# Cosformer attention and a mixer MLP on one core: program order by hand, batches in pairs of nine token chunks

## The chip, the cores and the metric

The kernel runs on one core of a Trainium2 chip. The metric is the device time of one launch in microseconds; the kernel before takes 447.08 us, the median of three runs (444.23 to 447.29). PE is TensorE (PEld its weight loads), DVE VectorE, ACT ScalarE, POOL GpSimd, and SP the engine whose queue issues every DMA of both kernels.

## The reference

Eight batches, eight heads, 576 tokens, head size 64; the model width is 512, the hidden width 2048, the rank 32. All inputs are float32.

```python
r = np.maximum(x, 0.0)                                   # phi of q and k
return np.concatenate([r * c, r * s], axis=-1)           # 64 -> 128 features
...
kv = np.einsum('bhsf,bhsd->bhfd', k_p, v)
z = np.sum(k_p, axis=2)
num = np.einsum('bhsf,bhfd->bhsd', q_p, kv)
den = np.einsum('bhsf,bhf->bhs', q_p, z)[..., None] + 1e-06
...
h = xt @ U @ V                                           # xt: x with tokens last
u = x + h.transpose(0, 2, 1)
ch = np.maximum(u @ w_ch1, 0.0) @ w_ch2
return (u + ch).astype(np.float32)
```

c and s are the cosine and sine of a token's angle, which depends on its position alone, and x is num/den with the heads side by side.

## The kernel before

Each batch is cut into five token chunks, four of 128 and one of 64. For a batch, `loads` fetches q, k and v of a chunk with one DMA each (tokens on partitions; every head of a token is a run of 64 floats, 256 bytes, in memory), casts v on POOL into `v_ext` with a column of ones (line 172), and writes the scaled relu of k and q on ACT, cosine and sine half apart (lines 173 to 185).

`front` is attention and low-rank mixing. For each chunk and head one PE transpose of q_p goes into a PSUM tile of 128x128 (line 218), which DVE copies out by itself (line 222). The state kv accumulates over chunks, four heads to a tile (line 236), and is cast by DVE (line 243). x is four matmuls of 65 columns (line 258); DVE adds 1e-6 to the four denominators and inverts them (lines 266 and 270), ACT scales the four heads one by one (line 273). A = U^T x is five matmuls of 512 columns (line 288), va = V^T A one per chunk (line 304); DVE adds x (line 308), and four transposes (line 314) with a DVE copy each (line 319) make uT.

`back` is the MLP. The first layer has 16 slices of the hidden width by two token groups of 288, four matmuls each (line 337), with the relu on ACT (line 344). The second layer takes a token chunk at a time, 16 matmuls of 512 columns (line 360), five chunks per batch, the last of 64 tokens; DVE adds u (line 368), and SP stores (line 372).

A scheduler sets the order on each engine from the order of the thunks and from dependencies. The main loop at the end mixes the thunks of `front(b)` evenly among those of `back(b - 1)`, with the loads of batch b + 1 after the 32nd thunk; in batch 0 the weight loads and their casts on ACT (lines 111 and 126) are mixed in instead. Transposes have two PSUM buffers, attention accumulators two, and a shared tag of four holds the other matmul outputs.

Of the kernel before, what the change touches and what calls it, by code (L numbers as in the profile page):

```python
# [17 lines left out]
def kernel(  # L18
# [13 lines left out]
    B = 8  # L32
    H = 8
    S = 576
    D = 64
    P = 128
    DM = 512
    DH = 2048
    R = 32

    nchunk = 5
    csz = [128, 128, 128, 128, 64]
    cst = [0, 128, 256, 384, 512]

    const_pool = ctx.enter_context(tc.tile_pool(name="const", bufs=1))
    wpool = ctx.enter_context(tc.tile_pool(name="w", bufs=1))
    bpool = ctx.enter_context(tc.tile_pool(name="bat", bufs=2))
    ps = ctx.enter_context(tc.tile_pool(name="ps", bufs=2, space=bass.MemoryType.PSUM))

    ident_bf = const_pool.tile([P, P], BF16)  # L50
    make_identity(nc, ident_bf)

    iota = const_pool.tile([P, nchunk], FP32)
    nc.gpsimd.iota(
        out=iota,
        pattern=[[128, nchunk]],
        base=0,
        channel_multiplier=1,
        allow_small_or_imprecise_dtypes=True,
    )  # L60
    cosang = const_pool.tile([P, nchunk, 1], FP32)
    sinang = const_pool.tile([P, nchunk, 1], FP32)
    scale_ang = math.pi / (2.0 * S)
    halfpi = const_pool.tile([P, 1], FP32)
    nc.vector.memset(halfpi, math.pi / 2.0)
    nc.scalar.activation(out=sinang, in_=iota, func=AF.Sin, bias=0.0, scale=scale_ang)
    nc.scalar.activation(
        out=cosang, in_=iota, func=AF.Sin, bias=halfpi, scale=-scale_ang
    )

    stgA = const_pool.tile([P, DH], FP32)
    stgB = const_pool.tile([P, DH], FP32)
    stgs = [stgA, stgB]
    w1_bf = wpool.tile([P, 4, DH], BF16)
    w2_bf = wpool.tile([P, 16, DM], BF16)
    stgV = const_pool.tile([R, S], FP32)
    V_bf = wpool.tile([R, S], BF16)
    stgU = const_pool.tile([P, nchunk, R], FP32)
    U_bf = wpool.tile([P, nchunk, R], BF16)

    def weight_thunks():
        thunks = []

        def mk_uv():
            def t():
                for c in range(nchunk):
                    nc.sync.dma_start(
                        out=stgU[: csz[c], c, :], in_=moe_U[cst[c] : cst[c] + csz[c], :]
                    )
                nc.sync.dma_start(out=stgV, in_=moe_V)  # L90
                for c in range(nchunk):
                    nc.scalar.activation(
                        out=U_bf[: csz[c], c, :],
                        in_=stgU[: csz[c], c, :],
                        func=AF.Copy,
                        bias=0.0,
                        scale=1.0,
                    )
                nc.scalar.activation(
                    out=V_bf, in_=stgV, func=AF.Copy, bias=0.0, scale=1.0  # L100
                )

            return t

        thunks.append(mk_uv())

        def mk_w1(d):
            def t():
                s = stgs[d % 2]
                nc.sync.dma_start(out=s, in_=moe_w_ch1[d * 128 : d * 128 + 128, :])  # L110
                nc.scalar.activation(
                    out=w1_bf[:, d, :], in_=s, func=AF.Copy, bias=0.0, scale=1.0
                )

            return t

        for d in range(4):
            thunks.append(mk_w1(d))

        def mk_w2(j):  # L120
            def t():
                s = stgs[j % 2]
                nc.sync.dma_start(
                    out=s[:, 0:DM], in_=moe_w_ch2[j * 128 : j * 128 + 128, :]
                )
                nc.scalar.activation(
                    out=w2_bf[:, j, :], in_=s[:, 0:DM], func=AF.Copy, bias=0.0, scale=1.0
                )

            return t  # L130

        for j in range(16):
            thunks.append(mk_w2(j))
        return thunks

    st_kp = [None] * B
    st_vext = [None] * B
    st_qp = [None] * B
    st_qpT = [None] * B
    st_x = [None] * B  # L140
    st_kv = [None] * B
    st_A = [None] * B
    st_u = [None] * B
    st_uT = [None] * B
    st_hidT = [None] * B

    def loads(b):
        k_p = bpool.tile([P, nchunk, H, 2 * D], BF16, tag="k_p")
        v_ext = bpool.tile([P, nchunk, H, D + 1], BF16, tag="v_ext")
        q_p = bpool.tile([P, nchunk, H, 2 * D], BF16, tag="q_p")  # L150
        st_kp[b] = k_p
        st_vext[b] = v_ext
        st_qp[b] = q_p
        thunks = [lambda: nc.vector.memset(v_ext[:, :, :, D : D + 1], 1.0)]

        def mk(c):
            sz = csz[c]
            st = cst[c]
            def t():
                q_st = bpool.tile([P, H, D], FP32, tag="q_st")  # L160
                k_st = bpool.tile([P, H, D], FP32, tag="k_st")
                v_st = bpool.tile([P, H, D], FP32, tag="v_st")
                nc.sync.dma_start(
                    out=q_st[:sz], in_=q[b].rearrange("h s d -> s h d")[st : st + sz]
                )
                nc.sync.dma_start(
                    out=k_st[:sz], in_=k[b].rearrange("h s d -> s h d")[st : st + sz]
                )
                nc.sync.dma_start(
                    out=v_st[:sz], in_=v[b].rearrange("h s d -> s h d")[st : st + sz]  # L170
                )
                nc.gpsimd.tensor_copy(out=v_ext[:sz, c, :, 0:D], in_=v_st[:sz])  # L172
                nc.scalar.activation(  # L173
                    out=k_p[:sz, c, :, 0:D], in_=k_st[:sz], func=AF.Relu,
                    bias=0.0, scale=cosang[:sz, c, :],
                )
                nc.scalar.activation(  # L177
                    out=k_p[:sz, c, :, D : 2 * D], in_=k_st[:sz], func=AF.Relu,
                    bias=0.0, scale=sinang[:sz, c, :],
                )  # L180
                nc.scalar.activation(  # L181
                    out=q_p[:sz, c, :, 0:D], in_=q_st[:sz], func=AF.Relu,
                    bias=0.0, scale=cosang[:sz, c, :],
                )
                nc.scalar.activation(  # L185
                    out=q_p[:sz, c, :, D : 2 * D], in_=q_st[:sz], func=AF.Relu,
                    bias=0.0, scale=sinang[:sz, c, :],
                )
            return t

        for c in range(nchunk):
            thunks.append(mk(c))
        return thunks

    def front(b):
        k_p = st_kp[b]
        v_ext = st_vext[b]
        q_p = st_qp[b]
        q_pT = bpool.tile([P, H, S], BF16, tag="q_pT", bufs=1)
        x_bf = bpool.tile([P, nchunk, DM], BF16, tag="x_bf", bufs=1)  # L200
        kv_sb = bpool.tile([P, H, D + 1], BF16, tag="kv", bufs=1)
        A_sb = bpool.tile([R, DM], BF16, tag="A_sb", bufs=1)
        u_bf = bpool.tile([P, nchunk, DM], BF16, tag="u_bf")
        uT = bpool.tile([P, 4, S], BF16, tag="uT")
        st_qpT[b] = q_pT
        st_x[b] = x_bf
        st_kv[b] = kv_sb
        st_A[b] = A_sb
        st_u[b] = u_bf
        st_uT[b] = uT  # L210
        thunks = []

        def mk_tr(c, h):
            sz = csz[c]
            st = cst[c]
            def t():
                tr_ps = ps.tile([P, P], BF16, tag="tr", bufs=2)
                nc.tensor.transpose(  # L218
                    out=tr_ps[:, :sz], in_=q_p[:sz, c, h, :],
                    identity=ident_bf[:sz, :sz],  # L220
                )
                nc.vector.tensor_copy(out=q_pT[:, h, st : st + sz], in_=tr_ps[:, :sz])  # L222
            return t

        for c in range(nchunk):
            for h in range(H):
                thunks.append(mk_tr(c, h))

        def mk_kv(hg):
            def t():  # L230
                acc = ps.tile([P, 4, D + 1], FP32, tag="acc", bufs=2)
                for i in range(4):
                    h = hg * 4 + i
                    for c in range(nchunk):
                        sz = csz[c]
                        nc.tensor.matmul(  # L236
                            out=acc[:, i, :],
                            lhsT=k_p[:sz, c, h, :],
                            rhs=v_ext[:sz, c, h, :],
                            start=(c == 0),  # L240
                            stop=(c == nchunk - 1),
# [206 lines left out]
```

## Time and profile before

| what | value |
|---|---|
| runs (us) | 447.08, 444.23, 447.29; median 447.08 |
| profiled execution, span from first to last instruction (us) | 442.4; its time outside the span is not reported |
| mean granted clock of TensorE | 0.984 |
| DMA packets | 121382, of which 114144 under 512 B; 46.79 MB |
| HBM read, written (MB) | 36.85, 9.44 |

The profile gives, for each engine, its busy time, and for each group of instructions the number, the mean duration and the idle time before them with what ended it. A duration of a matmul overlaps its neighbours, so what a matmul costs PE is read from start to start. The chain that ended last is followed back from the last instruction, each step to what released it.

### The profile page before, as it was taken

The numbers are of one execution on the slowest core, as the hardware profiler recorded it, in microseconds if no ns is written. First come the engines' busy times: TensorE is split into PE (matmuls) and PEld (weight loads), VectorE is DVE, ScalarE is ACT, GpSimd is POOL, SyncE is SP. The second block draws the span as 40 slices with busy tenths as digits, with TensorE's granted clock in tenths as the row PEclk, the third lists the DMA queues.
The fourth block names the chain that finished last, engine by engine and source line by source line (L and its number), as shares of the span: only waits on it lengthen the run. The fifth ranks groups of instructions, "written<-read, shape, count | busy, mean of one in ns | idle before, by whom it ended". The sixth has DMA issues, their size and how long they took to land.

```text
span 442.4 us, 7853 instructions
## 1 busy us (share of the span) xinstructions
PE 396.4 (90%) x2844; PEld 228.0 (52%) x2864; DVE 179.2 (41%) x753; ACT 276.3 (62%) x765; POOL 25.2 (6%) x47
## 2 busy tenths in 40 slices
PE   2754989829999999999999999999999999999995
PEld 1421665413675357644774357544764377535742
DVE  1524522314643464335643464335533564344011
ACT  6789699793499927991689338960575036702800
POOL 2100001110111001100110011000000000000000
PEclk9999999977999998999999999999999999999999
DMA  9757778873756665544541523131001100010011
GB/s 212 179 209 244 181 205 209 195 179 92 180 121 156 168 150 115 119 126 125 121 108 54 149 56 78 25 108 36 1 2 48 49 13 0 25 72 14 1 47 59
DMA packets 121382, 46.79 MB, mean 106 GB/s; under 512 B 114144, under 2 KB 114144, under 8 KB 120832
## 3 DMA queue, kind: packets, MB, share of 16 engines
q1 hardware_dynamic: 121344, 46.30, 40.6%
q8 instruction: 22, 0.36, 0.3%
q14 instruction: 16, 0.13, 0.1%
HBM read 36.85 MB, written 9.44 MB: 105 GB/s over the span
## 4 chain that ended last, share of the span: by engine, by line
PE 80%; ACT 11%; DVE 4%; DMA 3%; issue 2%; SPq 0%; DVEq 0%; ACTq 0%
PE o_ps L360 32%; PE g_ps L337 27%; PE acc L236 5%; PE tr_ps L218 5%; ACT x_bf L273 4%; PE trp L314 4%; PE acc L258 3%; PE va_ps L304 3%; DMA k_st<-in_k_dram 3%; PE A_ps L288 2%; ACT k_p L173 1%; ACT hidT L344 1%; ACT k_p L177 1%; ACT q_p L185 1%; ACT q_p L181 1%
## 5 line engine op out<-in xcount | busy, mean ns | idle before, releaser
L344 ACT ACTIVATE hidT<-g_ps 128x288 bf16<-128x288 f32 x256 | 101.5, 423 | 112.8 <-PE g_ps L337 106.8
L360 PE MATMUL o_ps<-w_bf,hidT 128*128 128x512 bf16 (+1 forms) x620 | 160.4, 384 | 1.0 <-issue 0.3
L337 PE MATMUL g_ps<-uT,w_bf 128*128 128x288 bf16 x1024 | 155.2, 291 | 1.7 <-ACT hidT L344 1.7
L337 PEld LDWEIGHTS <-w_bf 128*128 128x128 bf16 x1024 | 90.5, 99 | 27.9 <-issue 7.9
L222 DVE COPY q_pT<-tr_ps 128x128 bf16<-128x128 bf16 (+1 forms) x320 | 59.4, 215 | 79.9 <-PE tr_ps L218 78.8
L360 PEld LDWEIGHTS <-hidT 128*128 128x128 bf16 (+1 forms) x640 | 57.0, 100 | 60.9 <-issue 10.7
L273 ACT ACTIVATE x_bf<-acc,rec 128x64 bf16<-128x64 f32 (+1 forms) x320 | 74.3, 372 | 13.1 <-DVE rec L270 8.9
L218 PE MATMUL tr_ps<-ident_bf,q_p 128*128 128x128 bf16 (+1 forms) x320 | 53.9, 224 | 5.1 <-DVE q_pT L222 2.5
L368 DVE TENSOR_TENSOR o_sb<-u_bf,o_ps 128x512 f32<-128x512 bf16 (+1 forms) x40 | 27.3, 685 | 65.6 <-PE o_ps L360 54.3
L319 DVE COPY uT<-trp 128x128 bf16<-128x128 bf16 (+1 forms) x160 | 31.4, 215 | 30.1 <-PE trp L314 28.0
L218 PEld LDWEIGHTS <-q_p 128*128 128x128 bf16 (+1 forms) x320 | 29.7, 100 | 23.7 <-issue 13.7
L172 POOL CAST v_ext<-v_st 128x512 bf16<-128x512 f32 (+1 forms) x40 | 24.4, 615 | 244.8 <-DMA v_st<-in_v_dram 145.8
L258 PEld LDWEIGHTS <-q_pT 128*128 128x128 bf16 (+1 forms) x320 | 20.2, 104 | 34.1 <-issue 26.0
L258 PE MATMUL acc<-kv_sb,q_pT 128*128 128x65 bf16 (+1 forms) x320 | 24.5, 201 | 14.6 <-ACT x_bf L273 12.8
L314 PE MATMUL trp<-ident_bf,u_bf 128*128 128x128 bf16 (+1 forms) x160 | 31.1, 225 | 4.8 <-DVE uT L319 4.0
L181 ACT ACTIVATE q_p<-q_st,cosang 128x512 bf16<-128x512 f32 (+1 forms) x40 | 29.9, 748 | 7.0 <-DMA q_st<-in_q_dram 6.9
L173 ACT ACTIVATE k_p<-k_st,cosang 128x512 bf16<-128x512 f32 (+1 forms) x40 | 29.6, 739 | 6.7 <-PE trp L314 5.1
L266 DVE TENSOR_SCALAR rec<-acc 128x4 f32<-128x4 f32 (+1 forms) x80 | 12.7, 159 | 51.4 <-PE acc L258 50.8
L236 PE MATMUL acc<-v_ext,k_p 128*128 128x65 bf16 (+1 forms) x320 | 26.9, 204 | 7.0 <-POOL v_ext L172 6.9
L177 ACT ACTIVATE k_p<-k_st,sinang 128x512 bf16<-128x512 f32 (+1 forms) x40 | 29.8, 744 | 2.3 <-DMA k_st<-in_k_dram 2.3
L185 ACT ACTIVATE q_p<-q_st,sinang 128x512 bf16<-128x512 f32 (+1 forms) x40 | 29.7, 741 | 0.0
L236 PEld LDWEIGHTS <-k_p 128*128 128x128 bf16 (+1 forms) x320 | 19.3, 100 | 18.6 <-ACT k_p L173 6.1
(27 smaller groups left out, 124.6 us busy)
## 6 DMA issues: line engine op xcount, KB each, us to landing
q_st<-in_q_dram SPq DMA_DIRECT2D x32, 256.0 KB, 3.1
k_st<-in_k_dram SPq DMA_DIRECT2D x32, 256.0 KB, 3.4
v_st<-in_v_dram SPq DMA_DIRECT2D x32, 256.0 KB, 3.9
out_dram<-o_sb SPq DMA_DIRECT2D x32, 256.0 KB, 2.1
stgA<-in_moe_w_ch_dram SPq DMA_DIRECT2D x2, 1024.0 KB, 4.8
stgB<-in_moe_w_ch_dram SPq DMA_DIRECT2D x2, 1024.0 KB, 5.9
stgA<-in_moe_w_ch_dram SPq DMA_DIRECT2D x8, 256.0 KB, 2.9
stgB<-in_moe_w_ch_dram SPq DMA_DIRECT2D x8, 256.0 KB, 2.7
```

Of the source, the lines that this page charges most:

```text
L177: nc.scalar.activation(out=k_p[:sz, c, :, D : 2 * D], in_=k_st[:sz], func=AF.Relu, bias=0.0, scale=sinang[:sz, c, :],)
L181: nc.scalar.activation(out=q_p[:sz, c, :, 0:D], in_=q_st[:sz], func=AF.Relu, bias=0.0, scale=cosang[:sz, c, :],)
L185: nc.scalar.activation(out=q_p[:sz, c, :, D : 2 * D], in_=q_st[:sz], func=AF.Relu, bias=0.0, scale=sinang[:sz, c, :],)
L218: nc.tensor.transpose(out=tr_ps[:, :sz], in_=q_p[:sz, c, h, :], identity=ident_bf[:sz, :sz],)
L222: nc.vector.tensor_copy(out=q_pT[:, h, st : st + sz], in_=tr_ps[:, :sz])
L236: nc.tensor.matmul(out=acc[:, i, :], lhsT=k_p[:sz, c, h, :], rhs=v_ext[:sz, c, h, :], start=(c == 0), stop=(c == nchunk - 1),)
L258: nc.tensor.matmul(out=acc[:sz, i, :], lhsT=q_pT[:, h, st : st + sz], rhs=kv_sb[:, h, :], start=True, stop=True,)
L273: nc.scalar.mul(out=x_bf[:sz, c, h * D : h * D + D], in_=acc[:sz, i, 0:D], mul=rec4[:sz, i : i + 1],)
L314: nc.tensor.transpose(out=trp[:, :sz], in_=u_bf[:sz, c, d * 128 : d * 128 + 128], identity=ident_bf[:sz, :sz],)
L337: nc.tensor.matmul(out=g_ps, lhsT=w1_bf[:, d, j * 128 : j * 128 + 128], rhs=uT[:, d, g * gl : g * gl + gl], start=(d == 0), stop=(d == 3),)
L344: nc.scalar.activation(out=hidT[:, j, g * gl : g * gl + gl], in_=g_ps, func=AF.Relu, bias=0.0, scale=1.0,)
L360: nc.tensor.matmul(out=o_ps[:sz, :], lhsT=hidT[:, j, st : st + sz], rhs=w2_bf[:, j, :], start=(j == 0), stop=(j == 15),)
```

## The change

The kernel is written anew with `tc.manual_schedule()`: each engine runs its instructions in the order in which the program writes them.

- Tokens: a batch's first 512 tokens are laid out four to a partition (token 4p + c is row p of chunk c), so that a DMA run of q, k or v is 1 KB. Its last 64 tokens lie on partitions 0 to 63 for even batches and 64 to 127 for odd ones. Two batches make a pair with nine full chunks for the second layer, the ninth holding both tails. Loads are six DMAs per batch, batch 0's in halves of four heads.
- First layer: 512 token columns of a batch per matmul (`g1_main`), and per pair the 128 tail columns, four hidden slices to a PSUM tile (`g1_tail`).
- Evacuations: eight q transposes, or four of u, go into one tile and leave with one copy; the x normalisation of a chunk is one DVE multiplication for up to eight heads.
- Engines: the scaled relu of k on DVE, that of q on ACT, casts of the weights on POOL.
- PSUM tags: g three banks, o two, T one, X one tile of two banks.
- Order: batch 0's attention in two halves of heads, first layer of batch 0, attention of batch 1, then four pairs of 72 MLP slots each (pair 0 from slot 16), a slot being four matmuls of 512 columns or 16 of 128; attention of the next two batches stands at slots that a table gives.

On DVE, for a batch whose attention is spread in the middle of the run: q_pT is the transposed q, t_ps and tr_ps its PSUM tiles, rec the inverse denominators. Before:

```order
L222 COPY q_pT<-tr_ps 128x128 x32
L222 COPY q_pT<-tr_ps 128x64 x8
L266 TENSOR_SCALAR rec_1701<-acc 128x4
L270 RECIPROCAL rec_1701<-rec_1701 128x4
L266 TENSOR_SCALAR rec_1719<-acc 128x4
L270 RECIPROCAL rec_1719<-rec_1719 128x4
```

Now:

```order
L111 COPY q_pT<-t_ps 128x8x128
L263 TENSOR_SCALAR rec<-x_ps 128x8
L266 RECIPROCAL rec<-rec 128x8
L269 TENSOR_TENSOR x_bf<-x_ps,rec 128x512
L386 TENSOR_TENSOR o_sb<-u_bf,o_ps 128x512
L111 COPY q_pT<-t_ps 128x8x64
```

Forty copies became five, the scaling of x came over from ACT, and output additions stand between the steps.

On ACT, around the first layer of batch 0 (hidT and hid are the hidden activations, w_bf the cast weights). Before:

```order
L344 ACTIVATE hidT<-g_ps 128x288 x4
L173 ACTIVATE k_p<-k_st,cosang 128x8x64
L177 ACTIVATE k_p<-k_st,sinang 128x8x64
L344 ACTIVATE hidT<-g_ps 128x288 x3
L126 ACTIVATE w_bf<-stgA 128x512
L344 ACTIVATE hidT<-g_ps 128x288
```

Now:

```order
L109 ACTIVATE uT<-t_ps 128x4x128 x4
L109 ACTIVATE uT_tl<-t_ps 128x4x64
L339 ACTIVATE hid<-g_ps 128x512 x16
L182 ACTIVATE q_p<-qst,cosw 128x8x64
L182 ACTIVATE q_p<-qst,sinw 128x8x64
```

All sixteen activations of batch 0 stand ahead of the first q preparation of batch 1; k and the weights left the engine.

On SP, from the store of pair 0's ninth chunk on (kt, vt, qt are the tails, kst, vst, qst the main parts), only the new order:

```order
L389 DMA out_dram<-o_sb 64x512 x2
L77 DMA kt<-in_k_dram 64x8x64
L71 DMA kst<-in_k_dram 128x8x256
L77 DMA vt<-in_v_dram 64x8x64
L71 DMA vst<-in_v_dram 128x8x256
L77 DMA qt<-in_q_dram 64x8x64
L71 DMA qst<-in_q_dram 128x8x256
L393 DMA out_dram<-o_sb 128x512 x4
```

Batch 4's six loads wait in the queue behind the stores of slot 55.

The core of the diff:

```diff
-    nchunk = 5
-    csz = [128, 128, 128, 128, 64]
+    def tail(b):
+        lo = TS * (b % 2)
+        return slice(lo, lo + TS)
...
+    ctx.enter_context(tc.manual_schedule())
...
+    def load_main(dst, src, b, h0=0, h1=H, eng=None):
+        (eng or nc.sync).dma_start(
+            out=dst[:, h0:h1, :, :].rearrange("p h c d -> p h (c d)"),
+            in_=src[b, h0:h1, 0:512, :].rearrange("h (p c) d -> p h (c d)", c=4),
+        )
...
+            eng.tensor_scalar(
+                out=o, in0=i, scalar1=0.0, scalar2=w, op0=ALU.max, op1=ALU.mult
+            )
...
-                tr_ps = ps.tile([P, P], BF16, tag="tr", bufs=2)
...
-                nc.vector.tensor_copy(out=q_pT[:, h, st : st + sz], in_=tr_ps[:, :sz])
+        t_ps = ps.tile([P, H, P], BF16, tag="T", bufs=1, name="t_ps")
+        for h in range(h0, h1):
+            nc.tensor.transpose(
+                out=t_ps[:, h, 0:n], in_=q_p[b, c][rows, h, :], identity=ident[rows, rows]
+            )
+        cast(eng or nc.vector, q_pT[b][:, h0:h1, cols(c)], t_ps[:, h0:h1, 0:n])
...
-                for i in range(4):
-                    h = hg * 4 + i
-                    nc.scalar.mul(
-                        out=x_bf[:sz, c, h * D : h * D + D],
-                        in_=acc[:sz, i, 0:D],
-                        mul=rec4[:sz, i : i + 1],
-                    )
+        nc.vector.tensor_tensor(
+            out=dst.rearrange("p (g i d) -> p g i d", g=ng, d=D),
+            in0=view[:, :, :, 0:D],
+            in1=rec[rows].unsqueeze(3).to_broadcast([n, ng, 4, D]),
+            op=ALU.mult,
+        )
...
+    def g1_main(b, j):
...
+        g_ps = ps.tile([P, 512], FP32, tag="g", bufs=3, name="g_ps")
...
+    def g1_tail(pr, jq):
...
+    def g2_part(pr, cc, part):
...
+        if cc == 4:
+            lhs, c = hid_tl[pr], 0
+        else:
+            b, c = (2 * pr, cc) if cc < 4 else (2 * pr + 1, cc - 5)
+            lhs = hid[b]
+        for j in range(part * 4, part * 4 + 4):
+            nc.tensor.matmul(
+                out=o,
+                lhsT=lhs[:, j, c * P : c * P + P],
+                rhs=w2_bf[:, j, :],
...
+    def pe_plan(b):
+        plan = []
+        for c in range(5):
+            plan.append((2 * c, lambda c=c: qtr_unit(b, c)))
+        for hg in range(2):
+            plan.append((1 + 2 * hg, lambda hg=hg: kv_unit(b, hg, "X", 1)))
+        for c in range(5):
+            plan.append((5 + 2 * c + (2 if c == 4 else 0), lambda c=c: x_unit(b, c, (0, 1), "X", 1)))
+        plan.append((18, lambda: A_unit(b, "X", 1)))
+        for c in range(5):
+            plan.append((21 + 2 * c, lambda c=c: u_unit(b, c, "X", 1)))
+            plan.append((24 + 2 * c, lambda c=c: utr_unit(b, c)))
+        return plan
...
+    for hg in range(2):
+        h0 = 4 * hg
+        v_prep(0, h0, h0 + 4)
+        for c in (4, 0, 1, 2, 3):
+            k_prep(0, c, V_, h0, h0 + 4)
+            q_prep(0, c, A_, h0, h0 + 4)
...
+        kv_unit(0, hg, "g", 3)
+        for c in (4, 0, 1, 2, 3):
+            qtr_unit(0, c, h0, h0 + 4)
+            x_unit(0, c, (hg,), "o", 2)
...
+    for j in range(NJ):
+        g1_main(0, j)
+    for c in range(5):
+        k_prep(1, c, V_)
+        q_prep(1, c, A_)
...
+    for c in range(5):
+        qtr_unit(1, c)
+        x_unit(1, c, (0, 1), "X", 1)
+    A_unit(1, "o", 2)
+    for c in range(5):
+        u_unit(1, c, "o", 2)
+        utr_unit(1, c)
...
+            if pr == 0:
+                starts = (22, 47, 24)
+            else:
+                starts = (0, 37, 35)
+            for b, w in ((nb, starts[0]), (nb + 1, starts[1])):
...
+                    if b + 1 < B:
+                        put(w + 8, lambda b=b: load(b + 1))
+                for o, t in pe_plan(b):
+                    put(w + round(o * starts[2] / 36), t)
+            if pr + 2 < NPAIR:
+                for o, t in prep_plan(nb + 2):
+                    put(58 + o, t)
+                put(71, lambda nb=nb: load(nb + 3))
```

649 lines of the change are left out of this document (328 added, 321 removed).

## Prediction

> **What bounds the kernel now.** I read the shares by engine and the chain that ended last, then stretches, then the chain in order of time.
>
> ```profile
> span 442.4 us, 7853 instructions
> PE 396.4 (90%) x2844; PEld 228.0 (52%) x2864; DVE 179.2 (41%) x753; ACT 276.3 (62%) x765; POOL 25.2 (6%) x47
> PE 80%; ACT 11%; DVE 4%; DMA 3%; issue 2%; SPq 0%; DVEq 0%; ACTq 0%
> ```
>
> PE is 80% of the chain. Stretches show two regimes (columns: busy time of PE, PEld, DVE, ACT, POOL; clock, DMA share, GB/s).
>
> ```profile
> 0.00:11.00 11.00, 2.34 (x14) 1.31 (x15) 1.79 (x12) 6.93 (x12) 2.64 (x10) 1.00 0.94 212
> 22.00:33.00 11.00, 5.66 (x46) 3.27 (x46) 3.07 (x19) 8.84 (x27) 0.00 (x0) 1.00 0.59 207
> 242.00:300.00 58.00, 57.01 (x404) 31.36 (x408) 26.91 (x105) 36.08 (x102) 2.96 (x5) 1.00 0.31 80
> ```
>
> From about 110 us on PE has no holes; before that it waits for loads and for the chain of small attention steps. The chain in order of time gives the beat and the price of a streamed column.
>
> ```profile
> 242.27 0.97 PE A_ps L288 x4
> 290.34 0.97 PE A_ps L288 x4
> 405.55 15.05 PE g_ps L337 x122
> 420.87 10.74 PE o_ps L360 x49
> 438.02 0.68 DVE o_sb L368
> ```
>
> One batch takes 290.34 - 242.27 = 48.07 us. A 288-column matmul costs 15.05/122 = 0.1234, a 512-column one 10.74/49 = 0.219, the same 0.43 ns per column. After the last add 442.4 - 438.0 = 4.4 us are left for add and store.
>
> PE's timeline prices the rest, from start to start (a duration overlaps the next row).
>
> ```profile
> 254.46 0.23 PE L314 MATMUL trp<-ident_bf,u_bf 128*128 128x128 bf16 x1
> 254.62 0.40 PE L360 MATMUL o_ps<-w_bf,hidT 128*64 128x512 bf16 x1
> 254.95 0.23 PE L314 MATMUL trp<-ident_bf,u_bf 128*128 128x128 bf16 x1
> ...
> 258.51 1.01 PE L236 MATMUL acc<-v_ext,k_p 128*128 128x65 bf16 x14
> 259.36 0.27 PE L314 MATMUL trp<-ident_bf,u_bf 128*128 128x128 bf16 x2
> ...
> 264.41 0.28 PE L218 MATMUL tr_ps<-ident_bf,q_p 128*128 128x128 bf16 x2
> 264.52 0.65 PE L337 MATMUL g_ps<-uT,w_bf 128*128 128x288 bf16 x4
> ...
> 274.90 0.23 PE L218 MATMUL tr_ps<-ident_bf,q_p 64*128 64x64 bf16 x2
> 275.06 0.66 PE L337 MATMUL g_ps<-uT,w_bf 128*128 128x288 bf16 x4
> 275.66 0.23 PE L218 MATMUL tr_ps<-ident_bf,q_p 64*128 64x64 bf16 x2
> ...
> 279.02 0.29 PE L258 MATMUL acc<-kv_sb,q_pT 128*128 128x65 bf16 x4
> 279.15 0.65 PE L337 MATMUL g_ps<-uT,w_bf 128*128 128x288 bf16 x4
> ```
>
> A kv matmul costs 0.85/14 = 0.061, a 128-column transpose 0.055, an x matmul 0.033. Switching between a full and a half array is dear: transpose plus 64-row output matmul take 0.49 instead of 0.27, and a group with 64-row transposes takes 0.76 where 0.49 + 0.06 were due, so about 0.2 per switch. A batch at these prices is 128 x 0.1234 + 80 x 0.219 = 33.3, plus attention: 40 kv 2.4, 40 q transposes 2.2, 20 u transposes 1.1, 40 x 1.3, ten 512-column matmuls for A and va 2.2, together 9.2. That makes 42.5; the measured 48.07 holds 5.6 us of switches and short waits.
>
> **The change part by part.** Prices on the other engines (busy, mean ns):
>
> ```profile
> L344 ACT ACTIVATE hidT<-g_ps 128x288 bf16<-128x288 f32 x256 | 101.5, 423 | 112.8 <-PE g_ps L337 106.8
> L222 DVE COPY q_pT<-tr_ps 128x128 bf16<-128x128 bf16 x256 | 49.4, 222 | 58.3 <-PE tr_ps L218 57.3
> L181 ACT ACTIVATE q_p<-q_st,cosang 128x512 bf16<-128x512 f32 x32 | 24.1, 752 | 3.2 <-DMA q_st<-in_q_dram 3.2
> L308 DVE TENSOR_TENSOR u_bf<-x_bf,va_ps 128x512 bf16<-128x512 bf16 x32 | 21.1, 679 | 2.8 <-PE va_ps L304 2.8
> L172 POOL CAST v_ext<-v_st 128x512 bf16<-128x512 f32 x32 | 19.6, 616 | 225.8 <-DMA v_st<-in_v_dram 130.6 <-PE trp L314 69.2 <-PE o_ps L360 13.4
> L270 DVE RECIPROCAL rec<-rec 128x4 f32<-128x4 f32 x64 | 11.3, 178 | 2.0
> L266 DVE TENSOR_SCALAR rec<-acc 128x4 f32<-128x4 f32 x64 | 10.4, 162 | 40.6 <-PE acc L258 39.9 <-ACT x_bf L273 0.6
> L222 DVE COPY q_pT<-tr_ps 128x64 bf16<-128x64 bf16 x64 | 10.0, 188 | 21.6 <-PE tr_ps L218 21.6
> L243 DVE CAST kv_sb<-acc 128x260 bf16<-128x260 f32 x16 | 6.8, 428 | 7.4 <-PE acc L236 7.4
> ```
>
> *Nine chunks per pair.* The second layer falls from 160 to 144 matmuls per pair: 16 x 4 x 0.219 = 14.0 us less. The first layer keeps its columns; its 64 tail matmuls of 128 columns are taken at the kv price, 0.06. A pair is 128 x 0.219 + 64 x 0.06 + 144 x 0.219 = 63.4 us, attention adds 9.2 per batch plus four switches at the 64-row chunk, 0.8: 10.0. So a batch costs 63.4/2 + 10.0 = 41.7 instead of 48.07.
>
> *Wide evacuations.* From 128 to 64 columns a copy loses 34 ns, 0.53 ns per column, so 128x1024 costs 0.222 + 896 x 0.53 ns = 0.70 us; the upper bound is eight narrow ones, 1.5. The x normalisation leaves ACT for DVE: 0.16 + 0.18 + 0.68 = 1.02. The k preparation also moves to DVE, ten operations on 128x512 that no row shows; bounds 0.43 (the copy's slope) and 0.68 (the add), taken 0.55. DVE then carries per batch 5 x 0.70 + 2 x 0.43 + 5 x 1.02 + 11 x 0.68 (A, u, outputs) + 5 x 0.43 (uT) + 5.5 = 24.6 of 41.7 us. A hidden activation of 512 columns is 0.42 to 0.75 by the two ACT rows, below the 0.88 us of its four matmuls. Both hide behind PE.
>
> *Stalls left in the spread.* T has one buffer, X one of two banks. In pairs 1 and 2 units stand two MLP slots apart (1.75 us) and DVE answers in 0.70 or 1.02: nothing. In pair 0 they stand 1.3 slots apart and copies queue ahead of the x chain: 0.5 us on two x units per batch, 2 us. There ACT takes 10 q preparations between activations, 0.6 + 0.5 against 0.88: 1 us. SP issues batch 4's loads only after the store of slot 55, while DVE reaches its k preparation at slot 58, some 3.2 us later; loading k takes about 5, so DVE waits 2 us, and behind it uT copies and output adds, for which PE waits: 2 us. In pair 1, k preparation falls among the u additions: 2 us; pair 2: 1.
>
> *The start.* This term is unsure, and here nothing hides the chain.
>
> ```profile
> k_st<-in_k_dram SPq DMA_DIRECT2D x32, 256.0 KB, 3.4
> ...
> 19.99 3.13 PE acc L236 x32
> ...
> 40.19 1.86 PE L304 MATMUL va_ps<-A_sb,V_bf 32*128 32x512 bf16 x4 [0.77 <-DVE A_sb L295]
> ...
> 49.43 0.93 PE L337 MATMUL g_ps<-uT,w_bf 128*128 128x288 bf16 x3
> 53.02 0.65 PE L337 MATMUL g_ps<-uT,w_bf 128*128 128x288 bf16 x4
> ```
>
> Until about 53 us PE runs at half rate (three 288-column matmuls in 0.75-0.93, later four in 0.5-0.65), so kv costs 0.10 there, a 512-column matmul 0.46, a transpose 0.11. Loads in 1 KB runs lie between 212/0.94 = 226 GB/s (256 B runs) and 207/0.59 = 351 (8 KB rows); I take 280. The 1.3 MB ahead of the first kv land at 0.7 + 2 + 4.7 = 7.4, the v casts on POOL end at 9.5. Then: 20 kv 2.0 and cast 0.4 to 12; five chunks in series (copy 0.43, x 0.4, normalisation 0.8, hand-overs between engines 0.2: 1.8) to 21; a hand-over is an estimate of 0.1, below the copies' idle time of 58.3/256 = 0.23, which holds a transpose too; the k preparation of the other four heads, which DVE holds behind these chunks, 3 to 24; kv and five chunks again to 35.5; A and its cast to 37; five u chunks (va 0.46, add 0.68, four transposes 0.44, hand-overs 0.2: 1.8) to 46.5. POOL casts w1 in four pieces of 4 x 0.616 = 2.5 us, done by about 30: hidden, with 16 us to spare. First layer of batch 0: 64 x 0.219 = 14, plus 2 at half rate, to 62.5. Then comes all of attention 1 with no MLP beside it, because its q preparation stands on ACT behind the sixteenth activation: kv 2.5 to 4; tr 0.7; five chunks of copy 0.70, x 0.3 to 0.7, normalisation 1.02, hand-overs 0.3, together 2.3 to 2.55; A 1.4; five u chunks 1.5 to 1.8. Full rate gives 23.5, half rate 28.4. What drops the clock:
>
> ```profile
> 93.74 0.37 PE L258 MATMUL acc<-kv_sb,q_pT 128*64 128x65 bf16 x4 [4.48 <-ACT x_bf L273]
> ...
> 94.00:96.00 2.00, 1.38 (x11) 0.64 (x9) 0.65 (x4) 1.83 (x8) 0.49 (x1) 0.50 1.04 235
> ```
>
> After a hole of 4.48 us the granted clock was 0.50; attention 1 has holes of at most some 1.5 us, but many. I take 25.5, nearer the full rate. The Trainium skill, "TensorE: Matmul & The Clock Gate", Part 1 (the HAM clock gate), has the clock halve after an idle window of about 3.4 us; by that rule alone the stage keeps full rate and the sum is 2 us lower, at half rate 3 us higher. The trace agrees on the long hole and shows no stage of many short ones after a warm start. With 1 us of recovery pair 0 resumes at 89.
>
> *Sum.* 89 + pair 0 without batch 0's first layer (63.4 - 14 + 20 + 5 = 74.4) + pair 1 (83.4 + 2) + pair 2 (83.4 + 1) + pair 3 (63.4) + 4.4 = 401.0 of span. The median of the runs shown, 447.08, is 4.7 above the profiled span; with the same 4.7 the forecast is 406 us. As a check, eight batches at 48.07 and the ending leave 53 us of start in the kernel before; here the same subtraction leaves 55 besides 8 of stalls: the gain is the beat, not the start.
>
> **The rivals.** *A: DVE sets the pace (slower).* DVE takes its work in order, and k preparation, outputs, x and copies now share it, with one T and one X buffer. If PE waits at the 132 spread units (22 in each of six batches), it decides from 41/132 = 0.31 us per unit on. With a third of DVE's 24.6 us exposed in six batches: +49, 455 us. For it: pair 0's spacing. Against: DVE is needed 59% of the beat. 6%. The Trainium skill, "TensorE: Matmul & The Clock Gate", the table at its head, gives VectorE a strict FIFO, which is what lets one late operation hold all behind it; no run here shows VectorE out of order.
>
> *B: long start.* Loads at 226 GB/s, k preparation at 0.68, wide copies at 1.04 ns per column (the cast's slope, about 0.5 more on each of ten serial copies) and half rate in attention 1: 1 + 2 + 5 + 3, with w2 or batch 2 arriving late some 4 more: +15, 421 us. 16%.
>
> *C: short start, no stalls.* Loads at 351 GB/s, full rate from the second half on (kv, x and u chunks about 8 less in attention 0), 2 less in attention 1, 8 of stalls gone: -18, 388 us. For it: DVE's share; against: the half rate rows to 53 us. 15%.
>
> *D: PE's gain is not there*, because half-array switches and waits return at 5.6 per batch: 6 x 4.8 = 29, 435 us. 5%.
>
> **How the numbers follow.** Forecast 406: 58%, its own range 396 to 416. A measurement of this kernel tells about 1% from no change. B and C lie inside 384 to 430, the ends being C with a faster first load and B with a few more waits; A, D's upper part and a very slow start are outside. Faster by over 1% (below 442.6): all but A and the worst of B and D, 0.91; within 1%: 0.04; slower 0.05.
>
> **What would show it.** Right: o_ps matmuls 576 instead of 640; from the first g_ps matmul of pair 1 to that of pair 2 83 to 87 us; first g_ps matmul near 46, the first of batch 1 near 89; DVE's busy share 50 to 60%. Wrong: PE idle after 95 us ended by DVE copies or x (A), by DMA (B); a granted clock of 0.5 in the middle of pairs; first g_ps below 40 or above 55.

## The result, and the profile after

The changed kernel takes 414.58 us, the median of four runs (413.71 to 414.96), beside 446.06 (444.23 to 447.29) for the kernel before: ratio 0.928, 95% interval 0.924 to 0.932. The forecast of 406 was 8.6 us too low. (One execution of the ten-chunk kernel below took 1918.1 us, every matmul at about a sixth of its usual rate; it is left out of that kernel's numbers.)

First the page of the changed kernel: span, busy time by engine, shares of the chain, and the granted clock in 40 slices.

```profile
span 412.4 us, 6084 instructions
PE 362.8 (88%) x2544; PEld 183.9 (45%) x2544; DVE 183.8 (45%) x408; ACT 141.4 (34%) x242; POOL 45.7 (11%) x64
PEclk9999998559999996999999999999999999999999
PE 77%; DVE 14%; DMA 5%; issue 1%; SPq 1%; POOL 1%; DVEq 0%
```

PE is still the bound, with 33.6 us less busy time (396.4 to 362.8); DVE carries about as much as before (179.2 to 183.8) in 408 instructions instead of 753, ACT half of what it did. The clock row has two dents, at slices 7 to 9 (62 to 93 us) and 16 (155 to 165 us); both matter below.

The starts of the stages, from PE's timeline of the changed kernel (first layer of batch 0; attention 1; pair 0's next slot; pair 1):

```profile
48.09 16.37 PE L332 MATMUL g_ps<-uT,w_bf 128*128 128x512 bf16 x64
64.30 2.94 PE L219 MATMUL kv_ps<-v_ext,k_p 128*128 128x65 bf16 x40
91.06 7.60 PE L332 MATMUL g_ps<-uT,w_bf 128*128 128x512 bf16 x28
175.41 1.03 PE L332 MATMUL g_ps<-uT,w_bf 128*128 128x512 bf16 x4
```

And the end of the chain in order of time, where pair 3 runs alone:

```profile
346.19 27.63 PE g_ps L332 x128
373.82 3.57 PE gt_ps L350 x64
377.39 31.09 PE o_ps L375 x144
```

| stage | forecast | measured |
|---|---|---|
| to the first g_ps matmul | 46.5 | 48.1 |
| first layer of batch 0 | 16 | 16.2 |
| attention 1 | 25.5 and 1 of recovery | 26.8 |
| pair 0 from slot 16 | 74.4 | 84.4 |
| pair 1, pair 2 | 85.4, 84.4 | 85.6, 85.0 |
| pair 3 | 63.4 | 62.5 |
| ending | 4.4 | 3.9 |
| outside the span | 4.7 | 2.2 |

Pair 2 starts at 261.02, pair 3 at 346.03. One row of the table carries most of the miss: pair 0 is 10.0 us over. There DVE met a load that wasn't there; DVE's timeline of the changed kernel (the bracket is the idle time before a row and what ended it):

```profile
159.10 0.48 DVE L184 TENSOR_SCALAR k_p<-kst,cosw 128x512 bf16<-128x512 f32 x1 [7.02 <-DMA kst<-in_k_dram]
...
160.62 0.67 DVE L288 CAST A_sb<-a_ps 32x512 bf16<-32x512 f32 x1
```

SP's queue, and PE behind the A cast:

```profile
150.96 1.06 SPq L77 DMA_DIRECT2D kt<-in_k_dram  x1
152.07 0.62 SPq L71 DMA_DIRECT2D kst<-in_k_dram  x1
```

```profile
154.62 1.24 PE L375 MATMUL o_ps<-w_bf,hid 128*128 128x512 bf16 x5
161.35 0.58 PE L298 MATMUL va_ps<-A_sb,V_bf 32*128 32x512 bf16 x1 [5.48 <-DVE A_sb L288]
161.86 1.89 PE L375 MATMUL o_ps<-w_bf,hid 128*128 128x512 bf16 x4
```

DVE was free for batch 4's k preparation at 159.10 - 7.02 = 152.08, just when SP issued the load. The A cast of batch 3, which needs nothing from that load, stands behind it on DVE, and PE idles 5.48 us. Then four matmuls take 1.82 us (161.86 to 163.68) instead of 0.87: the hole has lowered the clock, as the stretches show (busy time of PE, PEld, DVE, ACT, POOL; clock; DMA share; GB/s).

```profile
150.00:158.00 8.00, 5.87 (x32) 2.26 (x31) 1.06 (x3) 0.00 (x0) 0.00 (x0) 1.00 0.79 204
160.00:164.00 4.00, 2.65 (x6) 0.53 (x5) 3.98 (x9) 0.00 (x0) 0.56 (x1) 0.50 1.14 275
```

### The profile page after: what moved, and what is told of

Read it like the earlier page. It is cut to its first block, busy times and chain, and to the rows that moved or that the text cites. A ratio compares the mean times of both kernels' runs of the same rounds, so it can differ in the third digit from the quotient of the medians.

```text
span 412.4 us, 6084 instructions
## 1 busy us (share of the span) xinstructions
PE 362.8 (88%) x2544; PEld 183.9 (45%) x2544; DVE 183.8 (45%) x408; ACT 141.4 (34%) x242; POOL 45.7 (11%) x64
## 4 chain that ended last, share of the span: by engine, by line
PE 77%; DVE 14%; DMA 5%; issue 1%; SPq 1%; POOL 1%; DVEq 0%
PE g_ps L332 28%; PE o_ps L375 25%; PE kv_ps L219 5%; PE x_ps L254 4%; PE gt_ps L350 4%; PE va_ps L298 3%; PE t_ps L238 3%; PE t_ps L318 3%; DVE k_p L184 3%; PE a_ps L281 2%; DMA out_dram<-o_sb 2%; DVE q_pT L111 2%; DVE x_bf L269 2%; DVE u_bf L301 2%; DMA kst<-in_k_dram 2%; DMA vst<-in_v_dram 1%
## 5 line engine op out<-in xcount | busy, mean ns | idle before, releaser
L375 PE MATMUL o_ps<-w_bf,hid 128*128 128x512 bf16 x512 | 124.1, 383 | 0.0
L332 PE MATMUL g_ps<-uT,w_bf 128*128 128x512 bf16 x512 | 123.8, 388 | 0.0
L339 ACT ACTIVATE hid<-g_ps 128x512 bf16<-128x512 f32 x128 | 76.5, 597 | 130.5 <-PE g_ps L332 130.5
L332 PEld LDWEIGHTS <-w_bf 128*128 128x128 bf16 x512 | 47.5, 100 | 53.8 <-issue 7.8
L375 PEld LDWEIGHTS <-hid 128*128 128x128 bf16 x512 | 45.7, 98 | 57.5 <-issue 13.4
L182 ACT ACTIVATE q_p<-qst,cosw 128x512 bf16<-128x512 f32 (+1 forms) x36 | 24.0, 665 | 64.5 <-DMA qst<-in_q_dram 41.7
L219 PE MATMUL kv_ps<-v_ext,k_p 128*128 128x65 bf16 (+1 forms) x320 | 26.1, 201 | 14.9 <-POOL v_ext L176 9.6
L111 DVE COPY q_pT<-t_ps 128x1024 bf16<-128x1024 bf16 (+2 forms) x45 | 26.1, 579 | 18.8 <-PE t_ps L238 18.4
L238 PE MATMUL t_ps<-ident,q_p 128*128 128x128 bf16 (+1 forms) x320 | 26.6, 229 | 0.6 <-DVE q_pT L111 0.6
L254 PEld LDWEIGHTS <-q_pT 128*128 128x128 bf16 (+1 forms) x320 | 15.5, 107 | 25.4 <-DVE q_pT L111 15.9
L182 ACT ACTIVATE q_p<-qst,sinw 128x512 bf16<-128x512 f32 (+1 forms) x36 | 23.9, 664 | 0.0
```

The source lines that it names most:

```text
L111: eng.tensor_copy(out=o, in_=i)
L182: nc.scalar.activation(out=o, in_=i, func=AF.Relu, bias=0.0, scale=w)
L219: nc.tensor.matmul(out=acc[:, i, :], lhsT=k_p[b][rows, c, h, :], rhs=vx[rows, c, h, :], start=(c == 0), stop=(c == 4),)
L238: nc.tensor.transpose(out=t_ps[:, h, 0:n], in_=q_p[b, c][rows, h, :], identity=ident[rows, rows])
L254: nc.tensor.matmul(out=acc[rows, g, i * E : i * E + E], lhsT=q_pT[b][:, h, cols(c)], rhs=kv_sb[b][:, h, :], start=True, stop=True,)
L332: nc.tensor.matmul(out=g_ps, lhsT=w1_bf[:, d, j * P : j * P + P], rhs=uT[b][:, d, :], start=(d == 0), stop=(d == 3),)
```

## The experiments

Each starts from the changed kernel (414.6 us) unless it says otherwise.

**The late k rows.**

```diff
-                    if b + 1 < B:
+                    if pr == 0 and b == nb + 1:
+                        put(45, lambda b=b: load_k(b + 1))
+                        put(51, lambda b=b: load(b + 1))
+                    elif b + 1 < B:
                         put(w + 8, lambda b=b: load(b + 1))
```

`load_k` allocates and issues the two DMAs of k; `load` then issues the rest.

> Batch 4's k rows (1 MB and the tail) are issued at slot 45 of pair 0 and its v and q rows at slot 51; in the changed kernel all of it is issued at slot 55, in the order k, v, q. My theory: the 7.0 us that DVE waited for these k rows at slot 58, with the A cast and PE's 5.5 us hole behind it and about 2.5 us of half clock after the hole, is the larger part of the 10 us by which pair 0 exceeded my sum. Then the whole goes from 414.6 to about 407 (405 to 409), DVE's wait for kst falls under 1 us, no hole over 1.5 us is left in PE between 150 and 170 us and the clock there stays at 1.0. Rival: the wait only changes its name (v or q rows, POOL's v casts, ACT's q preparation, or the outputs' stores behind the loads), then it gains 2 us at most.

Measured 407.64 us (407.25 to 408.27): 6.9 us less. Pair 0 from slot 16 takes 77.8 us instead of 84.4. DVE no longer waits for a load between 95 and 176 us, PE's longest wait there is 0.9, and the clock holds:

```profile
150.00:158.00 8.00, 8.00 (x41) 3.00 (x40) 6.28 (x15) 0.47 (x1) 4.76 (x5) 1.00 0.82 230
160.00:164.00 4.00, 3.30 (x19) 1.41 (x18) 2.43 (x6) 3.76 (x7) 0.00 (x0) 1.00 0.17 66
```

The theory holds; the rival, a wait with a new name, doesn't. Of the 3.4 us by which pair 0 still exceeds its forecast, some 1.4 are its first 28 matmuls, slowed by the clock that attention 1 leaves behind; that is the next experiment.

**The clock in attention 1.** The dent at 62 to 93 us has no long hole in it. PE's timeline of the changed kernel, then its stretches:

```profile
68.57 0.43 PE L254 MATMUL x_ps<-kv,q_pT 128*128 128x65 bf16 x8 [0.79 <-DVE q_pT L111]
68.84 0.61 PE L238 MATMUL t_ps<-ident,q_p 128*128 128x128 bf16 x8
70.82 0.62 PE L254 MATMUL x_ps<-kv,q_pT 128*128 128x65 bf16 x8 [1.37 <-DVE q_pT L111]
71.26 1.04 PE L238 MATMUL t_ps<-ident,q_p 128*128 128x128 bf16 x8
73.27 0.62 PE L254 MATMUL x_ps<-kv,q_pT 128*128 128x65 bf16 x8 [0.97 <-DVE q_pT L111]
...
75.71 0.62 PE L254 MATMUL x_ps<-kv,q_pT 128*128 128x65 bf16 x8 [0.97 <-DVE q_pT L111]
```

```profile
66.00:70.00 4.00, 2.67 (x41) 2.00 (x40) 2.27 (x6) 3.98 (x7) 2.45 (x5) 1.00 0.00 0
...
72.00:88.00 16.00, 9.94 (x64) 4.62 (x62) 9.33 (x20) 0.00 (x0) 2.07 (x4) 0.50 0.81 222
```

Eight transposes start to take longer after a hole of 0.79 and one of 1.37 us. The filler writes a PSUM tile that nobody reads:

```diff
+    def filler(n):
+        f_ps = ps.tile([P, 512], FP32, tag="g", bufs=3, name="f_ps")
+        for i in range(n):
+            nc.tensor.matmul(
+                out=f_ps, lhsT=w1_bf[:, i % 4, 0:P], rhs=uT[0][:, i % 4, :],
+                start=True, stop=True,
+            )
...
         qtr_unit(1, c)
+        filler(4)
         x_unit(1, c, (0, 1), "X", 1)
```

with four more before and after A and three between each va and its transposes.

> Matmuls of 512 columns that nobody reads (39 in all, 4 per x chunk and around A, 3 per u chunk) fill PE's holes in attention 1; all else stays, and the order of the real work too. My theory: the clock fell to 0.50 there because PE was busy for a third of the time only, in many short holes; with PE busy for over two thirds the clock stays above 0.8, x chunks take 2.25 instead of 2.44 us, u chunks 1.6 instead of 1.92, the stage 24 instead of 26.8, and the first slots after it run at full rate: 410 to 412. Rival: something else lowers the clock (half of it stays at 0.50), then the filler costs 0.43 us each and lies in the chain: stage 30 or more, 418 to 425.

Measured 410.08 us (409.53 to 410.70), with 43 such matmuls: doing more work on PE saved 4.5 us.

```profile
70.00:88.00 18.00, 16.06 (x124) 6.91 (x121) 11.85 (x28) 2.15 (x4) 0.23 (x1) 1.00 0.74 198
90.00:92.00 2.00, 2.00 (x11) 0.93 (x10) 2.00 (x5) 1.58 (x3) 0.74 (x2) 1.00 0.01 4
```

```profile
71.67 0.43 PE L254 MATMUL x_ps<-kv,q_pT 128*128 128x65 bf16 x8 [0.51 <-DVE q_pT L111]
73.92 0.43 PE L254 MATMUL x_ps<-kv,q_pT 128*128 128x65 bf16 x8 [0.52 <-DVE q_pT L111]
```

An x chunk takes 73.92 - 71.67 = 2.25 instead of 75.71 - 73.27 = 2.44, the stage 24.2 instead of 26.8, and pair 0's next 28 matmuls run at full rate. So many short holes were enough to bring the clock down, and filling them kept it up. The Trainium skill, "TensorE: Matmul & The Clock Gate", Part 1 (the HAM clock gate), names an idle window of about 3.4 us as what halves it; the trace disagrees, no hole before the fall being longer than 1.37 us.

What exactly is counted stays open. PE's share of busy time would fit these two stages, but not the kernel before, whose clock halved at 165.4 us, right after a stretch with PE busy for 88% of the time and no hole over 0.34 us:

```profile
162.00:165.40 3.40, 3.00 (x37) 2.00 (x36) 2.12 (x11) 1.20 (x2) 0.00 (x0) 1.00 1.01 227
165.40:168.80 3.40, 3.40 (x20) 2.38 (x18) 1.26 (x6) 1.24 (x3) 0.62 (x1) 0.51 1.06 240
```

Most matmuls of that stretch have 65 columns or 64 rows, so it may be the work done and not the busy time that counts; no run here tells the two apart.

**Attention 1 in the spread, and a warm start.** On top of the early k rows, attention 1 is put among MLP slots; batch 0's output slots come ahead of batch 1's first layer to make room.

```diff
+        if pr == 0:
+            slots = slots[0:16] + slots[36:52] + slots[16:36] + slots[52:72]
...
+            for o, t in pe_plan(1):
+                put(round(o * 24 / 36), t)
```

> On top of the run with the early k rows (407.6): attention 1 is spread like the others, over the 16 first-layer slots of batch 0 and eight of its output slots, which are moved ahead of batch 1's first layer; its k preparation and half of its q preparation stand on ACT during attention 0 and the first slots. My theory: the 26.8 us of attention 1 alone and 1.5 us of half clock after it become the 11.4 us that a batch's attention costs in the spread, less 2 to 4 us of new waits (units 1.3 slots apart, casts for w2): gain 11 to 15, 393 to 397. Rival: attention 1 is held by the loads of batch 1 or by ACT, which then has 10 preparations before the first slots, and the wait only moves ahead of the first slot: gain under 6, over 402.

Measured 391.84 us (391.18 to 392.89): 15.8 us less than 407.64, a little over the upper end. From the first g_ps matmul to pair 1's it takes 153.21 - 48.24 = 105.0 us instead of 120.9, and no slice of the clock row is under 9. PE's waits in that stretch, 48.3 to 153.2 us, sum to 4 us; the largest group (us in total, times, longest):

```profile
PE x_ps L254 <- DVE x_bf L269: 2.4, 6, 0.6
```

The last kernel adds, on top of that, filler to attention 0 (zeros, 320 columns: 28 ahead, 4 per chunk, 24 between the halves of heads, 10 around A); all five u chunks then use the X tile.

> On top of the run with attention 1 spread (391.8): matmuls of 320 zeros columns that nobody reads fill PE's holes in attention 0, from before the first kv to the first slot (28 ahead, 4 in each chunk, 24 between the head groups). Theory: the half rate of attention 0 (A matmuls 0.46, kv 0.10, the first eight of the first layer 0.43) is the state of a PE that has not been busy, although the granted clock reads 1.00 there; with the holes filled u chunks take 1.5 instead of 1.92, A 1.2 instead of 2.4, the first layer 2 less: -5 to -7, 385 to 387. Rival: the rate rises only later whatever PE does, then the filler costs 0.28 a piece in the chain, +5 or more.

Measured 385.83 us (384.38 to 386.46), ratio to the kernel before 0.865 (0.861 to 0.869): as expected. A's four matmuls and a u chunk show it; first the changed kernel, then this one.

```profile
35.49 1.89 PE L281 MATMUL a_ps<-x_bf,U_bf 128*32 128x512 bf16 x4
...
40.59 0.60 PE L298 MATMUL va_ps<-A_sb,V_bf 32*128 32x512 bf16 x1
42.51 0.60 PE L298 MATMUL va_ps<-A_sb,V_bf 32*128 32x512 bf16 x1
```

```profile
34.91 1.04 PE L281 MATMUL a_ps<-x_bf,U_bf 128*32 128x512 bf16 x4
...
38.52 0.39 PE L298 MATMUL va_ps<-A_sb,V_bf 32*128 32x512 bf16 x1
40.01 0.39 PE L298 MATMUL va_ps<-A_sb,V_bf 32*128 32x512 bf16 x1
```

A u chunk takes 1.49 instead of 1.92, and the first g_ps matmul starts at 44.40 instead of the 48.24 of the kernel without this filler.

**What spreading is worth.** All PE units of a batch's attention at one slot:

```diff
-                for o, t in pe_plan(b):
-                    put(w + round(o * starts[2] / 36), t)
+                for o, t in sorted(pe_plan(b), key=lambda e: e[0]):
+                    put(w + (8 if pr == 0 else 18 if b == nb else 16), t)
```

> The PE units of each later batch's attention stand together at one slot (in the order of before, at a slot where their buffers are free), instead of one to every one or two slots; preparation, loads and MLP stay. My theory: spreading is what hides the DVE answers: each of the six batches then costs as attention 1 did, 24 to 27 us in place of 11.4: +75 to +94, 490 to 508. Rival: the units wait for DVE in the spread as well and ACT or DVE bound it, then the order matters little: under 440.

Measured 491.80 us (490.67 to 492.89), slower than the kernel before. Pair 1 in the changed kernel and here:

```profile
175.41:261.02 85.61, 85.06 (x637) 43.65 (x636) 44.43 (x95) 33.83 (x56) 6.01 (x10) 1.00 0.39 112
```

```profile
193.01:307.55 114.54, 98.10 (x637) 49.15 (x636) 43.68 (x95) 33.83 (x56) 5.74 (x10) 0.84 0.30 83
```

The same instructions on every engine, DVE no busier, and 28.9 us more per pair: 15.9 of it PE idle, 13.0 slower matmuls at a mean clock of 0.84. That is 14.5 per batch, about what attention 1 costs over a batch in the spread, (85.0 - 62.5)/2 = 11.3: 26.8 - 11.3 = 15.5. The spread carries the change: with it, DVE's work is hidden, without it every answer is on the path.

**The ninth chunk.** The tail of a pair in the second layer as two halves of 64 rows:

```diff
+        halves = [slice(0, TS), slice(TS, P)] if cc == 4 else [slice(0, P)]
+        for hv in halves:
+            for j in range(part * 4, part * 4 + 4):
...
+                    out=o[hv, :],
+                    lhsT=lhs[:, j, c * P + hv.start : c * P + hv.stop],
```

> The tail chunk of a pair in the second layer is done again as two halves of 64 rows, one per batch (16 matmuls of 512 columns each, into the two halves of the same bank): 64 matmuls more in the whole, 640 as in the kernel before; the rest stays. My theory: a matmul costs its streamed columns, however few rows it fills, 64 x 0.217 = +13.9 us, and with switches between half and full array up to +17: 428 to 432. Rival: two matmuls on the two halves of the array overlap, or the time is hidden beside waits: within 4 us of 414.6, and the nine chunks gave nothing.

Measured 415.11 us, the median of its three ordinary executions (413.94 to 416.03): no 14 us. My theory fell. The same kernel once more, for its trace:

> The run with the tail chunk in two halves again (blocks of four matmuls into one half of the bank, then four into the other), because it came out at 414 to 416 and not at 428, for a trace of it at normal rate. New theory: the two halves use different columns of the array, so a block for one half runs beside a block for the other, and 32 matmuls take what 16 full ones take, 3.5 us per pair: 413 to 416 again, the o_ps matmuls of pair 3 still 31.1 us. Rival: the second 14 us are there but hidden by waits; then the o_ps matmuls of pair 3, where nothing else runs, take 34.5.

Measured 415.23 us (414.57 to 415.60). The other order, all 16 matmuls of one half first:

> As before, but all 16 matmuls of one half come first and then the 16 of the other, so that equal halves are neighbours. If neighbours on different halves run side by side, that is lost except at the one change: 3.2 us more per pair, +12 to +14, 426 to 429. If a matmul of 64 rows simply costs half, or PE reaches far ahead, it stays at 413 to 416.

Measured 423.85 us (422.31 to 424.80): 9.3 more than the changed kernel, where I had expected 12 to 14. Pair 3 of the two, alternating blocks first:

```profile
391.93 3.67 PE L377 MATMUL o_ps<-w_bf,hid_tl 128*64 128x512 bf16 x32
395.53 13.99 PE L377 MATMUL o_ps<-w_bf,hid 128*128 128x512 bf16 x64
```

```profile
396.39 6.26 PE L380 MATMUL o_ps<-w_bf,hid_tl 128*64 128x512 bf16 x32
402.59 9.67 PE L380 MATMUL o_ps<-w_bf,hid 128*128 128x512 bf16 x44
```

32 matmuls take 3.60 us when blocks of four change halves and 6.20 when they don't; 16 of 128 rows take 3.47 (16 x 0.217). In series 32 would take 6.94 (32 x 0.217); what is missing is the overlap at the one change of halves. So matmuls on different halves of the columns run side by side, and neighbours on the same half don't. The Trainium skill, "TensorEngine Tiling (Array Packing)", Tiling Modes (Key Properties), has different tiles of the array run in parallel; the trace agrees.

**Wide copies.** Cut up again, one copy per head or per 128 columns of u:

```diff
-        cast(eng or nc.vector, q_pT[b][:, h0:h1, cols(c)], t_ps[:, h0:h1, 0:n])
+        for h in range(h0, h1):
+            cast(eng or nc.vector, q_pT[b][:, h, cols(c)], t_ps[:, h, 0:n])
```

> The wide copies out of the transposes' bank are cut up again: 8 copies (one per head) for each q chunk and 4 for each u chunk; all else stays, so only DVE (and ACT in batch 0's u chunks) has more to do: 8 x 0.22 = 1.8 us in place of 0.69 per q chunk, 4 x 0.22 = 0.9 in place of 0.4 per u chunk, about 8 us per batch. My theory: with a unit at every second slot (1.75 us) this lies beside PE in pairs 1 and 2, and shows only where no MLP work runs beside attention: ten q chunks of four heads in attention 0 at 0.45 us, five of eight heads in attention 1 at 1.1, ten u chunks at 0.5, together +15 us, and some 3 more in pair 0 where units stand closer: 430 to 436. Rival (DVE is the bound in the spread too, since the next unit's bank comes free late): the 8 us per batch show in all eight batches: +50 to +64, 465 to 478. Second rival (copies overlap so well that their number doesn't matter): within 4 us of 414.6.

Measured 421.77 us (420.78 to 422.01): 7.2 more, less than half of what I expected, with DVE 23.7 us busier (207.5). Pairs 1 and 2 take 85.8 and 85.0 as before: free there, as expected. But the 15 us that I placed in attention 0 and 1 aren't there: the first g_ps matmul stands at 48.30, and attention 1 takes 27.4 instead of 26.8. The x matmuls no longer wait for the whole chunk; they start while the later copies still run. DVE, then PE, in attention 0 of this kernel:

```profile
31.49 0.60 DVE L111 COPY q_pT<-t_ps 128x128 bf16<-128x128 bf16 x4
```

```profile
31.75 0.64 PE L255 MATMUL x_ps<-kv,q_pT 128*128 128x65 bf16 x4 [0.63 <-DVE q_pT L111]
```

And four copies take 0.60, not 0.88. The loss is pair 0's, where units stand closest: 91.0 instead of 84.4, of which 3.1 are PE idle and 3.5 slower matmuls, at a mean clock of 0.91 instead of 0.94.

**Runs of 1 KB.** The same tokens fetched in runs of 256 bytes, four DMAs for one; and, as control, 1 KB runs with as many DMAs.

```diff
-            out=dst[:, h0:h1, :, :].rearrange("p h c d -> p h (c d)"),
-            in_=src[b, h0:h1, 0:512, :].rearrange("h (p c) d -> p h (c d)", c=4),
+                out=dst[:, h0:h1, c, :],
+                in_=src[b, h0:h1, 0:512, :].rearrange("h (p c) d -> c p h d", c=4)[c],
```

> The loads of q, k and v fetch runs of 256 B again (one DMA for each of a partition's four tokens, so four DMAs where one stood); token layout, order and everything else stay. My theory: the run's length sets the rate (226 GB/s for 256 B in the kernel before, 349 GB/s in the first 20 us of the changed one): the 1.3 MB ahead of the first kv come 2 us later, the second halves another 1 to 2, batch 4's k rows 2 to 3 later with the same hole in PE behind them: 418 to 423. Rival: the first stage is bound by DVE and the hand-overs, so the loads are hidden: 414 to 416.

> Control for the run with 256 B runs: runs of 1 KB as in the changed kernel, but each load is cut by heads into four DMAs, so that the number of DMAs is the same as there. My theory: what costs is the run's length, not the number of DMAs: 413 to 416. Rival (the issues on SP, about 0.6 us each, hold up the loads): as late as the run with 256 B, 418 to 423.

Measured 418.55 us (416.54 to 420.48) and 414.43 us (411.72 to 417.07). The size was right, the place wrong: with 256 bytes the first kv starts earlier (8.37 us, against 9.64, and 9.70 in the control), since each DMA now brings the token chunk that one preparation needs. The first g_ps matmul is 1.4 late all the same (49.45). The largest loss is in pair 1, 91.0 instead of 85.6, on DVE:

```profile
250.38 0.69 DVE L387 TENSOR_TENSOR o_sb<-u_bf,o_ps 128x512 f32<-128x512 bf16 x1 [4.32 <-DMA out_dram<-o_sb]
```

A store is held behind batch 6's loads on the same queue, its buffer isn't free, and DVE holds the u addition behind it. The control doesn't part run length from the number of DMAs cleanly: two of its four runs took 412 us and two 417, and the latter lie within the range of the 256-byte kernel.

**Grain.** Attention matmuls and the slot's matmuls alternate again:

```diff
+    def mm(fn):
+        fn()
+        calls[0] += 1
+        if mlp and calls[0] % 2 == 0:
+            mlp.pop(0)()
```

> The matmuls of each attention unit in the spread and those of the MLP slot ahead of it alternate (after every second attention matmul one of the slot's), as they stood in the kernel before in fine grain; units, slots and other engines stay, except that the slot's evacuation comes after the unit's. Theory: part of the 3.4 us per batch by which attention in the spread is cheaper than before (48.07 - 33.3 = 14.8 against 11.4) comes from fewer changes between full and partial array (64-row tail transposes, x of the tail, A with 32 columns, va with 32 rows): +1.5 to +3 per batch, 424 to 432. Rival: grain doesn't matter, the saving is in the waits: 412 to 417.

Measured 439.80 us (439.09 to 441.69), above my 424 to 432. Pairs 1 and 2 take 90.0 and 89.9, so 2.2 to 2.5 per batch, as expected; pair 0 takes 101.1, 16.7 us more, which I hadn't expected: PE's waits there are 13.2 us in all, 4.9 more, and the clock is down in six slices of the row instead of four. This kernel also evacuates a slot only after the attention unit beside it, so pair 0's loss isn't grain alone. Full and half array, in pair 2 of this kernel:

```profile
284.49 0.29 PE L255 MATMUL t_ps<-ident,q_p 128*128 128x128 bf16 x2
284.83 0.27 PE L255 MATMUL t_ps<-ident,q_p 128*128 128x128 bf16 x2
...
293.06 0.23 PE L255 MATMUL t_ps<-ident,q_p 64*128 64x64 bf16 x2
293.54 0.23 PE L255 MATMUL t_ps<-ident,q_p 64*128 64x64 bf16 x2
```

Two transposes and one matmul of 512 columns take 0.34 with the full array, the plain sum, and 0.48 with 64 rows, although those stream fewer columns.

## Why the prediction was right, and where it missed

*The beat (right).* A batch in pairs 1 and 2 costs 42.7 us, where I had 41.7 and stalls; pair 3 is within 1 us. The forecast's mechanism, PE with less work and no holes, is what the trace shows there: PE waits 0.6 us in pairs 1 and 2, against rival A; no 5.6 us per batch come back, against D. DVE is busy for 52% of pair 1 (44.43 of 85.61 us), but for 45% of the whole, below the 50 to 60% that I had named. Of the 5.4 us by which a batch got cheaper (48.07 to 42.7), the ninth chunk explains at most 1.2 (9.3/8) and the coarser grain 2.2 to 2.5; the rest was not taken apart.

*Nine chunks (right in sign, too large).* I priced the 64 dropped matmuls at 14.0 us. Against halves kept apart, the nearest run to the kernel before, they are worth 9.3; against alternating halves 0.6. I had not thought of two halves running together.

*Batch 4's loads (the step that failed).* The prediction had SP issue them 3.2 us ahead of DVE's need and load k in 5, "so DVE waits 2 us" and PE 2. From the first store of slot 55 (149.74) to DVE's arrival (152.08) it was 2.3 us, and SP spent them on issuing the two stores and the tail's DMA: it came to the k rows at 152.07, with no lead; the load took 7.0; DVE waited 7.02, PE 5.48, and about 2 us went to the lower clock. A granted clock of 0.50 in the middle of a pair, which I had named as a sign of being wrong, did appear here. Early k rows gave 6.9 us back.

*Attention 1 (mis-sized).* I took 25.5, between full and half rate, and 1 us of recovery, and wrote that the trace of before agrees with the rule of one long hole; I had overlooked its fall at 165.4 us, which has none. The trace of the changed kernel has half rate from 70 us on, 26.8, and 1.4 for the first 28 matmuls; the filler brings 24.2, near my 23.5 at full rate.

*The start.* The first g_ps matmul was 1.6 us late: k preparation 1.8 late, kv and x chunks 1.0 faster than priced, A 0.8 slower. Of the 1.8, 1.7 are one operation (last section).

*The margin* (luck). Outside the span it was 2.2, not 4.7, which hid 2.5 us of these misses: with 2.2 the forecast would have been 403.2, 11.4 too low. The 4.7 was not time outside the span; it set the median of the runs against a profile of a faster execution. In every run on record time and span differ by 1.7 to 2.0 us.

## What to carry to other kernels

When an in-order engine serves several batches, a load needed by a later batch must be issued well ahead of its first reader, since the wait stops all that stands behind it; read the lead as the time from the queue's issue to the engine's arrival, not as a count of slots, and set it against the load's time to landing. Short serial stages on PE cost twice, by their waits and by the clock that falls behind them: put other work between them, and where there is none, matmuls that nobody reads can pay. Before a half-filled matmul is counted as waste, see whether its neighbour uses the other half of the array.

## What the runs showed of the hardware

The granted clock in the record does not tell the rate of the start: between 34 and 44 us it reads 1.00 in the changed kernel, while A's matmuls take 0.46 us each and not 0.217. In the warm start the row reads 0.50 from 12 to 18 us and 0.80 from 18 to 20, and agrees with the matmuls' rate from there.

A DVE operation from float32 in SBUF and a cast on POOL held each other up. In the changed kernel, DVE and then POOL:

```profile
21.99 0.34 DVE L184 TENSOR_SCALAR k_p<-kst,cosw 128x256 bf16<-128x256 f32 x1
22.26 2.01 DVE L184 TENSOR_SCALAR k_p<-kst,sinw 128x256 bf16<-128x256 f32 x1
```

```profile
22.05 2.08 POOL L111 CAST w_bf<-wst 128x2048 bf16<-128x2048 f32 x1 [0.39 <-DMA wst<-in_moe_w_ch_dram]
```

The operation of 0.34 us takes 2.01 and ends about when the cast does. In the control with more DMAs the cast came 0.8 us later, no k preparation took over 0.34, POOL's two casts took 5.00 us together instead (1.89 each where nothing stood beside them), and the first g_ps matmul stood at 46.49. Nothing was done to that stage but to cut its loads, so it seems that 1.6 us hang on which of the two comes first; that alone was not tried.
